# Chunk 0 of a banded-attention and gated-FFN kernel: the second head of each pair is normalized on GpSimd, the first on VectorE

## The chip, the cores and the metric

The kernel runs on one core of one Trainium2 chip. The metric is device time in microseconds (us) of one execution, the median of several runs. The engines are TensorE (PE, with weight loads shown as PEld), VectorE (DVE), ScalarE (ACT), GpSimd (POOL) and SyncE (SP), which issues the loads.

## The reference

Two layers follow each other, all in float32. The first is attention with a narrow band and block summaries: batch 4, 8 heads, 768 positions, head size 64.

```python
k_sum = k.reshape(B, H, nb, block, D).max(axis=3)      # block = 32, nb = 24
v_sum = v.reshape(B, H, nb, block, D).mean(axis=3)
mask_l = np.abs(pos[:, None] - pos[None, :]) < window   # window = 16
scores_l_m = np.where(mask_l, scale * q @ k.T, -1e9)
scores_s = scale * np.einsum('bhsd,bhnd->bhsn', q, k_sum) + np.log(block)
scores_all = np.concatenate([scores_l_m, scores_s], axis=-1)
a = np.exp(scores_all - scores_all.max(-1, keepdims=True))
a = a / (np.sum(a, axis=-1, keepdims=True) + 1e-09)
attn = np.matmul(a, np.concatenate([v, v_sum], axis=2))
```

The second is a feed-forward layer on the eight heads side by side (512 wide, inner width 1024): `h = relu(x @ w_in)`, a convolution of three taps along the positions, a sigmoid gate, and `(h * gate) @ w_out`.

## The kernel before

**Tiling.** The 4 x 768 positions are cut into 8 chunks of 384 (two to a batch element). In a chunk the 8 heads form 4 pairs, so there are 32 pairs, numbered n; pairs 0 to 3 are chunk 0, pairs 4 to 7 chunk 1. A pair goes through `qk` (scores of 64 queries against 96 banded keys and 24 block maxima, in PSUM tiles `pq`), `softmax`, `tr` (each head's scores `a` are transposed on TensorE into the single PSUM tile `pt`, which is copied to SBUF as `aT`) and `av` (product with the values into `xp`, which is split into a high and a low part, `xh` and `xl`).

**Softmax.** For each head and each of three blocks VectorE adds the mask and takes the row maximum (L278), and ScalarE takes the exponential with its row sum (L288). ScalarE then adds 1e-9 to the six sums (L296), VectorE inverts them (L297), and each head's 128 x 360 scores are multiplied by the inverse (L300): the normalization. `n >= NP` sends it to GpSimd from pair 4 on; in chunk 0 VectorE does both heads.

**Feed-forward.** x and both weights are held as a high and a low float32r part, so a product is three matmuls (`f1`, L404; `f2`, L473). `unit` does one of eight slices of the inner width for a chunk: `f1`, then `gate_conv` and `gate_mul`.

**Weights.** They arrive as 64-bit words and are decoded at the start of the kernel: for each of eight blocks of `w_in` (w0 to w7 here) ScalarE scales the high word (L97), VectorE does three integer steps (L100, L101, L104), ScalarE rounds the result to `win_hi` (L127) and GpSimd subtracts it for `win_lo` (L128). The decoded words live in a ring of three buffers `wu`, so L97 of block i waits for L128 of block i-3. In the order listings wu_485, 493, 606, 614, 627, 635, 701 and 709 are w0 to w7.

**Order.** SyncE's loads of chunk 0 follow the list `LOADS`. In chunks 0 and 1 (`ORDERED = 2`) the order of instructions on each engine is set by a scheduler with a cost model of its own, which places all engines' instructions of these chunks; from chunk 2 on TensorE's order is the written one. Within an engine instructions run strictly in order, so an instruction that waits holds all behind it. In chunk 0 matmuls on an idle tile (`warm`, `pw`, L78) fill TensorE's gaps.

Of the kernel before, what the change touches and what calls it, by code (L numbers as in the profile page):

```python
# [25 lines left out]
NP = H // 2  # L26
# [24 lines left out]
def attention_ffn(ctx, tc, qT, kT, vT, v4, w_in, cwT, w_out, mask8, ident_in, out):  # L51
    nc = tc.nc
# [195 lines left out]
    def qk(c, p):  # L248


        st = state[(c, p)]
        n = c * NP + p
        pq = [
            ps.tile([P, 512], F32, tag="s", name=f"pq{n}_{h}", bufs=2) for h in range(2)
        ]
        for blk in range(CB):
            i, half = divmod(blk, 2)
            for h in range(2):
                r = slice(h * QB, (h + 1) * QB)
                last = nc.tensor.matmul(  # L260
                    pq[h][half * QB : (half + 1) * QB, i * NK : (i + 1) * NK],
                    st["q"][r, blk * QB : (blk + 1) * QB],
                    st["kw"][r, blk, :],
                    start=True,
                    stop=True,
                )
        if c == 0:
            warm(f"pq{p}", ins(last))
        softmax(n, c % 2, pq)

    def softmax(n, hf, pq):
        nm = sp.tile([P, 2, 3], F32, tag="nm", name=f"nm{n}", bufs=3)
        sm = sp.tile([P, 2, 3], F32, tag="sm", name=f"sm{n}", bufs=3)
        for h in range(2):
            a = sp.tile([P, 3, NK], F32, tag="a", name=f"a{n}_{h}", bufs=DEPTH + 2)
            state[("a", 2 * n + h)] = a
            for i in range(3):
                nc.vector.tensor_tensor_reduce(  # L278
                    a[:, i, :],
                    pq[h][:, i * NK : (i + 1) * NK],  # L280
                    mask[:, hf, i, :],
                    -0.125,
                    3.0e38,
                    ALU.add,
                    ALU.min,
                    nm[:, h, i : i + 1],
                )
                nc.scalar.activation(  # L288
                    a[:, i, :],
                    a[:, i, :],  # L290
                    AF.Exp,
                    bias=nm[:, h, i : i + 1],
                    scale=-1.0,
                    accum_out=sm[:, h, i : i + 1],
                )
        nc.scalar.activation(sm, sm, AF.Copy, bias=1e-9)  # L296
        nc.vector.reciprocal(sm, sm)  # L297
        for h in range(2):
            a = state[("a", 2 * n + h)]
            (nc.gpsimd if n >= NP else nc.vector).tensor_tensor(  # L300
                a, a, sm[:, h, :].unsqueeze(2).to_broadcast([P, 3, NK]), ALU.mult
            )

# [187 lines left out]
    for item in LOADS.split():  # L491
        what, n = item[0], int(item[1:] or 0)
# [193 lines left out]
```

## Time and profile before

| | us |
|---|---|
| median of 3 runs | 405.03 (401.72 to 405.11) |
| the profiled execution | 405.19 |
| span in its profile | 403.3 |
| TensorE busy | 387.8 (96%) |
| VectorE busy | 262.9 (65%) |
| ScalarE busy | 255.8 (63%) |
| GpSimd busy | 150.3 (37%) |

The span runs from the first to the last instruction; 1.9 us of the execution lie outside it. Busy shares are means over stages with different limits; of TensorE's busy time part is `warm` matmuls, whose results nobody reads.

### The profile page before, as it was taken

What the parts mean: (1) busy time and instruction counts of PE and PEld (TensorE: products, weight loads), DVE (VectorE), ACT (ScalarE), POOL (GpSimd) and SP (SyncE); (2) the same over time, 40 slices, a digit from 0 to 9 for tenths busy, and PEclk for the clock granted to TensorE, in tenths of its full rate; (3) what the DMA queues carried; (4) which work ended last, traced back from release to release, by engine and by line L of the source; (5) the groups of instructions that cost most, each with busy time, mean ns of one, the idle gap of its engine ahead of it and who ended that gap; (6) DMA issues with size and microseconds to landing.
All of it is one profiled execution on the core that took longest, in us unless ns stands there. A gap on an engine that the chain in (4) does not pass through costs nothing.

```text
span 403.3 us, 8835 instructions
## 1 busy us (share of the span) xinstructions
PE 387.8 (96%) x3173; PEld 322.2 (80%) x3173; DVE 262.9 (65%) x777; ACT 255.8 (63%) x806; POOL 150.3 (37%) x179
## 2 busy tenths in 40 slices
PE   8989879999989999999999999999999999999996
PEld 3546558787768888888888888888888888999884
DVE  4889969998976665667765466466565655556200
ACT  3575699998876787766666778666666653343211
POOL 2316565377764234332333333332422242222200
PEclk9999799999899999999999999999999999999999
DMA  8999783666896784546233343334220000000011
GB/s 293 337 367 191 203 212 119 210 199 194 237 205 188 229 261 127 150 148 199 68 101 112 79 114 113 101 98 120 67 63 28 28 2 26 26 28 27 28 52 52
DMA packets 60715, 54.47 MB, mean 135 GB/s; under 512 B 24640, under 2 KB 51328, under 8 KB 60672
## 3 DMA queue, kind: packets, MB, share of 16 engines
q1 hardware_dynamic: 56928, 47.19, 41.2%
q10 hardware_dynamic: 3744, 6.73, 4.5%
q8 instruction: 25, 0.41, 0.5%
q14 instruction: 18, 0.15, 0.1%
HBM read 45.55 MB, written 6.29 MB: 129 GB/s over the span
## 4 chain that ended last, share of the span: by engine, by line
PE 85%; ACT 5%; DVE 3%; DMA 3%; POOL 2%; issue 1%; SPq 0%; DVEq 0%; POOLq 0%
PE f L473 33%; PE f L404 32%; PE pq L260 7%; PE xp L329 5%; PE pt L308 5%; PE pw L78 3%; ACT a L288 2%; DMA va<-v 2%; DMA k_xh<-kT 1%; POOL wout_lo L128 1%; DVE a L300 1%; POOL glo L456 0%; ACT wu_o L97 0%; ACT t L425 0%; PE pv L234 0%
## 5 line engine op out<-in xcount | busy, mean ns | idle before, releaser
L456 POOL TENSOR_TENSOR glo<-t,ghi 128x383 fp32r<-128x383 f32 (+1 forms) x64 | 66.3, 1037 | 138.3 <-ACT ghi L455 125.9
L404 PE MATMUL f<-xh,win_hi 128*128 128x384 f32 (+1 forms) x256 | 92.5, 361 | 0.9 <-ACT win_hi L127 0.9
L434 DVE SCALAR_TENSOR_TENSOR t<-f,cw,t 128x382 f32<-128x382 f32 (+3 forms) x128 | 78.8, 615 | 19.2 <-ACT t L425 16.6
L404 PE MATMUL f<-xl,win_hi 128*128 128x384 f32 (+1 forms) x256 | 87.9, 344 | 0.0
L404 PE MATMUL f<-xh,win_lo 128*128 128x384 f32 (+1 forms) x256 | 87.2, 341 | 0.0
L288 ACT ACTIVATE a<-a,nm 128x120 f32<-128x120 f32 x192 | 73.4, 384 | 12.3 <-DVE nm L278 12.1
L473 PE MATMUL f<-wout_lo,ghi 128*128 128x512 f32 x192 | 75.7, 394 | 1.6 <-POOL wout_lo L128 1.6
L473 PE MATMUL f<-wout_hi,ghi 128*128 128x512 f32 x192 | 76.4, 398 | 0.0
L473 PE MATMUL f<-wout_hi,glo 128*128 128x512 f32 x192 | 75.0, 391 | 0.0
L300 POOL TENSOR_TENSOR a<-a,sm 128x360 f32<-128x360 f32 x56 | 45.7, 837 | 45.6 <-ACT f L422 28.1
L451 ACT ACTIVATE t<-t 128x383 f32<-128x383 f32 (+1 forms) x64 | 33.6, 526 | 40.3 <-DVE t L434 39.6
L452 DVE SCALAR_TENSOR_TENSOR t<-t,f 128x383 f32<-128x383 f32 (+1 forms) x64 | 35.2, 552 | 29.6 <-ACT t L451 29.6
L404 PEld LDWEIGHTS f<-xh,win_hi 128*128 128x128 f32 x256 | 49.3, 192 | 5.1 <-ACT win_hi L127 1.2
L404 PEld LDWEIGHTS f<-xl,win_hi 128*128 128x128 f32 x256 | 49.2, 192 | 1.4 <-issue 0.3
L404 PEld LDWEIGHTS f<-xh,win_lo 128*128 128x128 f32 x256 | 48.9, 191 | 0.2
L278 DVE CUSTOM_DVE_ANT_0 a<-pq,mask 128x120 f32<-128x120 f32 x192 | 42.7, 275 | 1.5 <-PE pq L260 1.3
L473 PEld LDWEIGHTS f<-wout_lo,ghi 128*128 128x128 f32 x192 | 36.1, 188 | 7.9 <-POOL wout_lo L128 2.2
L473 PEld LDWEIGHTS f<-wout_hi,glo 128*128 128x128 f32 x192 | 36.1, 188 | 7.7
L473 PEld LDWEIGHTS f<-wout_hi,ghi 128*128 128x128 f32 x192 | 36.2, 188 | 7.0 <-issue 0.5
L315 ACT COPY aT<-pt 120x384 f32<-120x384 f32 x60 | 28.2, 470 | 20.7 <-PE pt L308 20.7
L422 ACT ACTIVATE f<-f 128x384 f32<-128x384 f32 (+1 forms) x64 | 30.4, 475 | 15.8 <-PE f L404 15.6
L308 PE MATMUL pt<-ident,a 128*120 128x128 f32 x192 | 33.7, 283 | 5.1 <-ACT aT L315 3.1
(59 smaller groups left out, 508.8 us busy)
## 6 DMA issues: line engine op xcount, KB each, us to landing
va<-v SPq DMA_DIRECT2D x32, 288.0 KB, 4.2
kw<-kT SPq DMA_DIRECT2D x28, 288.0 KB, 6.4
q<-qT SPq DMA_DIRECT2D x32, 192.0 KB, 4.5
out_dram<-ob ACTq DMA_DIRECT2D x24, 256.0 KB, 2.0
kT<-kT SPq DMA_DIRECT2D x12, 392.0 KB, 3.9
vt<-vT SPq DMA_DIRECT2D x12, 384.0 KB, 4.3
wo<-w_out SPq DMA_DIRECT2D x8, 512.0 KB, 5.3
raw_a<-w_in SPq DMA_DIRECT2D x6, 512.0 KB, 11.5
```

The costliest lines, as they stand in the source:

```text
L260: last = nc.tensor.matmul(pq[h][half * QB : (half + 1) * QB, i * NK : (i + 1) * NK], st["q"][r, blk * QB : (blk + 1) * QB], st["kw"][r, bl ...
L278: nc.vector.tensor_tensor_reduce(a[:, i, :], pq[h][:, i * NK : (i + 1) * NK], mask[:, hf, i, :], -0.125, 3.0e38, ALU.add, ALU.min, nm[:, h ...
L288: nc.scalar.activation(a[:, i, :], a[:, i, :], AF.Exp, bias=nm[:, h, i : i + 1], scale=-1.0, accum_out=sm[:, h, i : i + 1],)
L300: (nc.gpsimd if n >= NP else nc.vector).tensor_tensor(a, a, sm[:, h, :].unsqueeze(2).to_broadcast([P, 3, NK]), ALU.mult)
L308: last = nc.tensor.transpose(pt[:NK, i * P : (i + 1) * P], a[:, i, :], ident)
L404: last = nc.tensor.matmul(ph[:, :n], w[:, fc, cc, :], x[:, cc, :n], start=(cc == 0 and m == 0), stop=(cc == NCC - 1 and m == 2),)
L422: nc.scalar.activation(h[:, :n], h[:, :n], AF.Relu)
L434: nc.vector.scalar_tensor_tensor(t[:, i0:i1], h[:, hf + k - 1 + i0 : hf + k - 1 + i1], cw[:, fc, k : k + 1], t[:, i0:i1], ALU.mult, ALU.add,)
L451: nc.scalar.activation(t, t, AF.Tanh, scale=0.5)
L452: nc.vector.scalar_tensor_tensor(t, t, 1.0, h[:, hf : hf + ng], ALU.add, ALU.mult)
L456: nc.gpsimd.tensor_tensor(gated["lo"][:, fc, d0 : d0 + ng], t, hi.bitcast(F32), ALU.subtract)
L473: nc.tensor.matmul(po, gx[:, fc, ss], w[:, fc, :], start=(fc == 0 and m == 0), stop=(fc == NFC - 1 and m == 2),)
```

## The change

In `softmax` the test that picks the engine of the normalization gets `or h`: in chunk 0, too, GpSimd now multiplies the scores of the second head (h = 1) of each pair. That is four instructions. Nothing else is edited.

```diff
         for h in range(2):
             a = state[("a", 2 * n + h)]
-            (nc.gpsimd if n >= NP else nc.vector).tensor_tensor(
+            (nc.gpsimd if n >= NP or h else nc.vector).tensor_tensor(
                 a, a, sm[:, h, :].unsqueeze(2).to_broadcast([P, 3, NK]), ALU.mult
             )
```

The scheduler reacts to it with another order of both ordered chunks on every engine. Three places matter below.

ScalarE, between the second and the fourth pair of chunk 0, before (a_0_364 and a_1_371 are the two heads of pair 3, wu_i_485 and wu_i_493 are w0 and w1):

```order
L315 COPY aT_307<-pt_301 120x384
L296 ACTIVATE sm_275<-sm_275 128x6
L236 ACTIVATE vm_2_298<-pv_2_296 24x128
L349 CAST xh_325<-xp_309 128x384
L97 ACTIVATE cw<-cw_words 128x24
L97 ACTIVATE wu_i_485<-raw_a 128x512
L97 ACTIVATE wu_i_493<-raw_a 128x512
L288 ACTIVATE a_0_364,sm_363<-a_0_364,nm_362 128x120 x3
L288 ACTIVATE a_1_371,sm_363<-a_1_371,nm_362 128x120 x3
```

The same place on ScalarE now:

```order
L296 ACTIVATE sm_275<-sm_275 128x6
L315 COPY aT_307<-pt_301 120x384
L97 ACTIVATE wu_i_493<-raw_a 128x512
L349 CAST xh_325<-xp_309 128x384
L97 ACTIVATE wu_i_606<-raw_a 128x512
L127 CAST win_hi<-wu_i_493 128x512
L97 ACTIVATE wu_i_614<-raw_a 128x512
L236 ACTIVATE vm_3_386<-pv_3_384 24x128
L288 ACTIVATE a_0_364,sm_363<-a_0_364,nm_362 128x120 x3
L288 ACTIVATE a_1_371,sm_363<-a_1_371,nm_362 128x120 x3
```

The exponentials of pair 3 stood behind the first step of w0 and w1; now they stand behind that of w1, w2 and w3 and behind the finished w1.

VectorE, ahead of the first masked maximum of pair 4 (a_0_540), before:

```order
L344 CAST xl_748<-xl_326 128x4x2
L101 SCALAR_TENSOR_TENSOR wu_i_614<-wu_i_614,wl_i_615 128x512
L104 SCALAR_TENSOR_TENSOR wu_i_614<-raw_a,wu_i_614 128x512
L100 TENSOR_SCALAR wl_i_628<-raw_a 128x512
L101 SCALAR_TENSOR_TENSOR wu_i_627<-wu_i_627,wl_i_628 128x512
L104 SCALAR_TENSOR_TENSOR wu_i_627<-raw_a,wu_i_627 128x512
L100 TENSOR_SCALAR wl_i_636<-raw_a 128x512
L278 ISA a_0_540,nm_538<-pq_0_524,mask 128x120
```

VectorE at the same place now (xp_462 is the attention output of pair 3):

```order
L104 SCALAR_TENSOR_TENSOR wu_i_635<-raw_a,wu_i_635 128x512
L100 TENSOR_SCALAR wl_i_702<-raw_b 128x512
L101 SCALAR_TENSOR_TENSOR wu_i_701<-wu_i_701,wl_i_702 128x512
L350 TENSOR_TENSOR xl_326<-xp_462,xh_325 128x384
L104 SCALAR_TENSOR_TENSOR wu_i_701<-raw_b,wu_i_701 128x512
L100 TENSOR_SCALAR wl_i_710<-raw_b 128x512
L344 CAST xh_747<-xh_325 128x4x2
L344 CAST xl_748<-xl_326 128x4x2
L101 SCALAR_TENSOR_TENSOR wu_i_709<-wu_i_709,wl_i_710 128x512
L278 ISA a_0_540,nm_538<-pq_0_524,mask 128x120
```

Before, w0 to w4 and the first step of w5 were decoded when pair 4's softmax began; now w0 to w6 and two steps of w7 are.

GpSimd in the first half of chunk 0, before and now in one piece of the difference (va are the values' block means, kw_107 the keys of pair 3, the ISA row loads a function library):

```order
 L217 COPY kw_100<-ks_243 128x6x24
 L238 COPY va_104<-vm_0_175 24x768
+L300 ISA
+L300 TENSOR_TENSOR a_1_160<-a_1_160,sm_152 128x360
+L300 TENSOR_TENSOR a_1_217<-a_1_217,sm_209 128x360
+L238 COPY va_111<-vm_1_232 24x768
+L238 COPY va_116<-vm_2_298 24x768
 L213 COPY kw_107<-k_xl 128x6x96
-L238 COPY va_111<-vm_1_232 24x768
 L217 COPY kw_107<-ks_331 128x6x24
```

The two normalizations and two copies of block means now stand ahead of pair 3's keys; the library load, which stood ahead of the first L128, now stands ahead of the first L300.

## Rows read from the trace of the kernel before

**Rows 1.** The page: its head, part 1 (busy us, share, instructions), and the granted clock of part 2 in 40 slices.

```profile
span 403.3 us, 8835 instructions
PE 387.8 (96%) x3173; PEld 322.2 (80%) x3173; DVE 262.9 (65%) x777; ACT 255.8 (63%) x806; POOL 150.3 (37%) x179
...
PEclk9999799999899999999999999999999999999999
```

**Rows 2.** Busy time of each engine in stretches of 10 us, then the granted clock (1.00 is 2.4 GHz), the DMA share and GB/s.

```profile
40.00:50.00 10.00, 8.05 (x61) 5.53 (x51) 9.21 (x33) 6.12 (x29) 5.78 (x5) 0.74 0.70 197
50.00:60.00 10.00, 7.06 (x96) 5.44 (x95) 6.77 (x28) 9.11 (x30) 5.69 (x7) 0.92 0.85 222
60.00:70.00 10.00, 10.00 (x95) 8.09 (x94) 9.26 (x29) 9.35 (x32) 5.93 (x8) 1.00 0.38 119
...
100.00:110.00 10.00, 9.45 (x56) 7.43 (x57) 10.00 (x24) 8.60 (x27) 7.47 (x7) 0.83 0.84 220
```

**Rows 3.** TensorE in order of time: start, duration, operation, count, and in brackets the idle time ahead and what ended it.

```profile
43.54 0.83 PE L260 MATMUL pq<-kw,q 64*64 64x120 f32 x12 [1.95 <-issue]
...
59.74 0.52 PE L308 MATMUL pt<-ident,a 128*120 128x128 f32 x3 [2.79 <-ACT aT L315]
...
60.80 0.44 PE L404 MATMUL f<-xh,win_hi 128*128 128x384 f32 x1
...
101.75 0.50 PE L473 MATMUL f<-wout_lo,ghi 128*128 128x512 f32 x1 [0.54 <-POOL wout_lo L128]
...
111.95 0.50 PE L473 MATMUL f<-wout_lo,ghi 128*128 128x512 f32 x1 [1.03 <-POOL wout_lo L128]
```

**Rows 4.** The normalization by line: engine, count, ns shortest/median/longest, first and last start.

```profile
L300 POOL TENSOR_TENSOR a<-a,sm x56: 777/790/1333, 46.8 to 325.5; 128x360 f32<-128x360 f32 x56
L300 DVE TENSOR_TENSOR a<-a,sm x8: 521/604/1153, 12.6 to 28.8; 128x360 f32<-128x360 f32 x8
```

**Rows 5.** VectorE in order of time: the four pairs of normalizations of chunk 0, and the first masked maximum of pair 3.

```profile
12.63 1.64 DVE L300 TENSOR_TENSOR a<-a,sm 128x360 f32<-128x360 f32 x2
...
17.26 1.12 DVE L300 TENSOR_TENSOR a<-a,sm 128x360 f32<-128x360 f32 x2
...
21.72 1.60 DVE L300 TENSOR_TENSOR a<-a,sm 128x360 f32<-128x360 f32 x2
...
24.18 0.27 DVE L278 CUSTOM_DVE_ANT_0 a<-pq,mask 128x120 f32<-128x120 f32 x1
...
28.35 0.97 DVE L300 TENSOR_TENSOR a<-a,sm 128x360 f32<-128x360 f32 x2
```

**Rows 6.** VectorE in order of time: the three steps of one undisturbed block of weights, the instructions that took longer than their like, the split of pair 3's attention output (L350), and the first masked maximum of pair 4.

```profile
30.30 0.42 DVE L100 TENSOR_SCALAR wl_i<-raw_a 128x512 uint32<-128x512 uint32 x1
30.76 0.69 DVE L101 SCALAR_TENSOR_TENSOR wu_i<-wu_i,wl_i 128x512 uint32<-128x512 uint32 x1
31.48 0.69 DVE L104 SCALAR_TENSOR_TENSOR wu_i<-raw_a,wu_i 128x512 uint32<-128x512 uint32 x1
...
33.70 1.65 DVE L101 SCALAR_TENSOR_TENSOR wu_i<-wu_i,wl_i 128x512 uint32<-128x512 uint32 x1
...
35.99 0.55 DVE L350 TENSOR_TENSOR xl<-xp,xh 128x384 fp32r<-128x384 f32 x1
...
36.79 0.16 DVE L344 CAST xh<-xh 128x8 fp32r<-128x8 f32 x1
36.87 1.28 DVE L344 CAST xl<-xl 128x8 fp32r<-128x8 f32 x1
...
40.63 1.65 DVE L104 SCALAR_TENSOR_TENSOR wu_i<-raw_a,wu_i 128x512 uint32<-128x512 uint32 x1
...
42.65 0.27 DVE L278 CUSTOM_DVE_ANT_0 a<-pq,mask 128x120 f32<-128x120 f32 x1
```

**Rows 7.** GpSimd in order of time over the same stretch.

```profile
31.57 3.24 POOL L128 TENSOR_TENSOR win_lo<-wu_i,win_hi 128x512 fp32r<-128x512 f32 x2 [3.11 <-ACT win_hi L127]
...
36.80 1.31 POOL L128 TENSOR_TENSOR win_lo<-wu_i,win_hi 128x512 fp32r<-128x512 f32 x1 [1.29 <-ACT win_hi L127]
...
40.19 1.54 POOL L128 TENSOR_TENSOR win_lo<-wu_i,win_hi 128x512 fp32r<-128x512 f32 x1 [1.29 <-DMA va<-v]
```

**Rows 8.** ScalarE in order of time: the copy of pair 3's first transposed head, then from the first exponential of pair 4 to the copy that frees `pt` at 59.6 us.

```profile
30.42 0.48 ACT L315 COPY aT<-pt 120x384 f32<-120x384 f32 x1 [2.00 <-PE pt L308]
...
42.96 0.40 ACT L288 ACTIVATE a<-a,nm 128x120 f32<-128x120 f32 x1
...
49.92 0.48 ACT L315 COPY aT<-pt 120x384 f32<-120x384 f32 x1 [2.23 <-PE pt L308]
...
50.41 0.61 ACT L127 CAST win_hi<-wu_i 128x512 fp32r<-128x512 f32 x1
50.91 0.48 ACT L422 ACTIVATE f<-f 128x384 f32<-128x384 f32 x1
52.28 0.48 ACT L315 COPY aT<-pt 120x384 f32<-120x384 f32 x1 [0.89 <-PE pt L308]
...
53.13 0.62 ACT L127 CAST win_hi<-wu_i 128x512 fp32r<-128x512 f32 x1
53.64 0.70 ACT L97 ACTIVATE wu_i<-raw_b 128x512 f32<-128x512 f32 x1
...
59.11 0.49 ACT L315 COPY aT<-pt 120x384 f32<-120x384 f32 x1
```

## The prediction

> **What bounds the kernel now.** I read the page's head first: TensorE is busy for 387.8 of 403.3 us, and its granted clock is below 0.9 in two of the 40 slices only [rows 1]. So a saving must take idle time, `warm` matmuls or slow-clock time from TensorE; work taken off another engine counts only through these. The table of 10 us stretches tells where that is possible [rows 2]. From 60 us on TensorE is full (10.00 of 10); between 40 and 60 it has 8.05 and 7.06, and the granted clock, 0.74 and 0.92, says that part of that time ran at the 1.2 GHz level. The four moved instructions lie before this point, so the question is when TensorE gets past it. I take the matmul group on `pt` at 59.74 as the checkpoint: behind it stands the first wide feed-forward matmul, at 60.80, and after that TensorE is fed nearly without a gap [rows 3]. A shift of the checkpoint is a shift of the end, unless something later gives it back.
>
> What sets the checkpoint? The matmul at 59.74 waits for ScalarE's copy of 59.11, the last of a chain on ScalarE that begins with pair 4's first exponential at 42.96 [rows 8]. That one needs pair 4's first masked maximum, which VectorE runs at 42.65 as the next item of a full queue (9.21 of 10 us busy between 40 and 50) [rows 2, 6]. So: VectorE's queue up to 42.65, then ScalarE's chain, then the checkpoint.
>
> **The change part by part.**
>
> *Relief.* The four pairs of normalizations cost VectorE 1.64 + 1.12 + 1.60 + 0.97 = 5.33 us [rows 5]. Half goes: -2.7 us.
>
> *Order.* The listing of VectorE now has more decoding ahead of pair 4's maximum: two steps of w5 (0.69 + 0.69 less overlap, 1.3), all three of w6 (1.8) and two of w7 (1.2), by the three durations of an undisturbed block [rows 6]: +4.3 us.
>
> *Interference.* Three instructions took far longer than their like while GpSimd was at an L128: 1.65 for 0.69 (33.70), 1.28 for 0.16 (36.87), 1.65 for 0.69 (40.63), together 3.0 us [rows 6]; GpSimd worked 3.24 + 1.31 + 1.54 = 6.1 us there [rows 7]. VectorE lost half of GpSimd's time. In the new order six L128 at about 1.3 us (7.8) and four normalizations at 0.79 (3.2) [rows 4, 7] come before pair 4's maximum, 11.0 us, half of which is 5.5: +2.5 over before. The bounds are no loss beyond today's (0) and the loss of all 11.0 us (+8). I take the half, because it is what this stage shows.
>
> VectorE's own sum: 42.65 - 2.7 + 4.3 + 2.5 = 46.75, between 44.25 and 52.25.
>
> *A second path to the same place.* The split of pair 3's output (L350) now stands ahead of pair 4's maximum, so VectorE also waits for pair 3. Pair 3's maximum was at 24.18 [rows 5]. Ahead of it now are w0, w1 and two steps of w2 (3.6 + 1.2 = 4.8); three pairs' relief is -2.2, and interference from one L128 and three normalizations (1.3 + 3 x 0.79, halved) is +1.8: 28.6. From there to pair 3's normalization I keep roughly the distance of before (28.35 - 24.18 = 4.2), with 1.2 for the larger ScalarE queue, in which the exponentials stand behind the first step of w1 to w3: 34.0. From normalization to L350's end took 36.5 - 28.35 = 8.2 us [rows 5, 6], which gives 42.2. But the copy of the first transposed head, 2.1 us behind the normalization before (30.42) [rows 8], now stands on ScalarE behind the first step of w6, which waits in the ring for GpSimd's L128 of w3. That is 34.0 + 0.5 + 0.8 + 0.3 for GpSimd to reach it, two L128 at 1.3 and 0.7 for the step itself (L97 took 0.70 [rows 8]): 38.9, and 39.4 with the copy, 3.3 later than its old distance. So L350 ends at 45.5. Behind it stand the last of w6, two steps of w7 and the casts, 2.0 us, and half an L128, 0.65: **pair 4's maximum at 48.1**. The later of the two paths counts, 5.5 us behind 42.65.
>
> *What ScalarE gives back.* From pair 4's first exponential to the copy's end it took 59.60 - 42.96 = 16.64 us. Of that, 2.23 + 0.89 were waits for TensorE [rows 8], which a later start absorbs. Two L127 (0.61, 0.62), the L422 and an L97 (0.70) stood in between; they were done earlier or come later in the new order, about 2.1 us net of overlap. That leaves 11.4. The checkpoint is then 48.1 + 0.3 + 11.4 + 0.14 = 59.9, against 59.74: +0.2. Pair 4's score tiles and `pt` are shared by alternating pairs, and such hand-overs have left gaps of 1.95 and 2.79 us on TensorE [rows 3]; I allow a part, 0.8. **Front: +1.0 us.**
>
> *Middle.* In chunk 1 the new order puts the first `f2` matmuls behind unit 3, whose 12 `f1` matmuls take some 2.1 us. The waits for `wout_lo` of 0.54 and 1.03 [rows 3] are then mostly covered: -0.8. At best the slow clock there goes too (9.45 us busy at 0.83 [rows 2], so 1.7 us) and it is -3.3; if the moved unit waits itself, +1.
>
> *Costs taken at nothing.* The library load moves from before the first L128 to before the first L300. Its time shows in no row; it lies between 0 and the 3.11 us that GpSimd waited there anyway [rows 7]. Now the first head's transposition, behind a matmul on block means that comes later, covers it; without that cover up to 3 us of pair 0 are lost, ahead of VectorE's queue and so mostly absorbed there. The second head's 0.79 us on GpSimd runs beside VectorE's half, and a pair took 0.97 to 1.64 on VectorE alone [rows 4, 5]: no later. SyncE's loads keep their list.
>
> **Sum.** 405.19 (the profiled execution, 0.16 above the median, 1.9 of it outside the span) + 1.0 - 0.8 = **405.4 us**.
>
> *Where a page speaks against it.* A normalization took 777 to 1333 ns on GpSimd and 521 to 1153 on VectorE, by the medians 790 to 604, a ratio of 1.3 [rows 4]. The Trainium skill, "GPSIMD Engine Reference", section 4.1 (Engine selection), puts elementwise work with two inputs at about twice VectorE's time. By that the four would take some 1.2 us more on GpSimd than I count, and half of that, 0.6 us, would return to VectorE (an estimate from that page); the measured 790 ns decides here.
>
> **The rivals.**
>
> *A. Slower: GpSimd's instructions hold VectorE for their whole length.* The place is VectorE's queue up to pair 4's maximum; the price is the upper bound above, 52.25, then 0.3 + 11.4 + 0.14: checkpoint 64.1, +4.4, so 409.6 without the middle's gain. It decides once VectorE loses over 9 of the 11 us. For it: each of the three long instructions is an elementwise one that ran beside an L128. Against it: other instructions ran at their usual length in GpSimd's 6.1 us, and only half was lost [rows 6, 7]. By the Trainium skill, "SBUF — State Buffer", section "SBUF: two separate sides", the two engines share a port pair under an exclusive lock, held for a whole instruction, with the loser blocked. The three long rows agree with that; the ordinary ones between them show that not every VectorE instruction asks for it. Chance 0.15.
>
> *B. Faster: the relief gets through.* Were the interference no more than before and pair 3 in time, pair 4's maximum comes at 44.25 and the checkpoint at 44.25 + 0.3 + 11.4 + 0.14 = 56.1, -3.6 us; with the middle 400.8, at best 398.3. For it: 2.7 us really leave a queue that is full. Against: the decoding moved ahead of it is larger, and the ring's wait behind pair 3 is new. Chance 0.13.
>
> *C. Slower by the clock.* Between 40 and 50 us, with idle stretches such as the 1.95 at 43.54, TensorE was granted 0.74 [rows 2, 3]. If the later pair 4 moves such a stretch into 50 to 60, where 7.06 us ran at 0.92, the work there takes about 3 us longer with no gap to absorb it: 405.4 + 3 = 408.4. Chance 0.10.
>
> That the change does not do what it says is out: the listings show the four instructions on GpSimd.
>
> **How the numbers follow.** My forecast has 0.62, A 0.15, B 0.13, C 0.10. One per cent, 4 us, is about what a measurement of this kernel can tell from no change. Faster than 401.0: most of B and a little of the forecast with the middle's best end, 0.14. Slower than 409.1: most of A, part of C and the forecast's tail if the interference is nearer its upper bound, 0.24. Within: 0.62. The range runs from 401.0, just above B, to 409.4, just below A, and leaves out about 2 in 10.
>
> **What would show it.** On VectorE four L300 instead of eight before 50 us, pair 4's first maximum near 48 (44 is B, 52 is A), and more L101, L104 or casts of over 1.2 us. On ScalarE an L97 waiting for GpSimd's L128 just before pair 3's `aT`. On TensorE the `pt` group that waits for `aT` near 60, the clock of 50 to 60 near 0.92 (C: 0.7), and smaller waits for `wout_lo` after 100. I would be wrong if the block of w_in decoding takes much longer through the ring than its parts (each step waits for another engine), if pair 3's weights for ScalarE arrive late and hold its exponentials, or if the new order of chunk 1 opens gaps on TensorE after 60 us, which the rows of before cannot show.

## The result and the profile after

The changed kernel takes 406.39 us (median of 20 runs, 405.68 to 407.16), the kernel before 404.94 in the same comparison (20 runs, 401.41 to 406.59). The ratio is 1.0057, with a 95% interval of 1.0035 to 1.0079: slower by half a per cent, inside the 1% that the forecast (405.4) called no change, and inside its range. In every comparison, executions more than 1.5% above the fastest of the same kernel count as slow and are left out of the ratio. The profiled execution took 405.68 us, so the profiles stand 0.5 us apart and the medians 1.45.

The page of the changed kernel, its head, part 1 and the granted clock of part 2:

```profile
span 403.8 us, 8837 instructions
PE 384.4 (95%) x3163; PEld 319.4 (79%) x3173; DVE 262.6 (65%) x773; ACT 256.5 (64%) x806; POOL 152.9 (38%) x183
...
PEclk9999999999999999999999999999999999999999
```

Against [rows 1], four instructions have gone from DVE (777 to 773) to POOL (179 to 183), and TensorE is busy 3.4 us less in a span 0.5 us longer. The ten matmuls fewer are records that this trace lacks, all of `warm` (75 against 85, with 3173 weight loads in both), so part of the 3.4 us is theirs. What differs where, the 10 us stretches tell (PE, PEld, DVE, ACT, POOL busy, then granted clock, DMA share, GB/s):

```profile
10.00:20.00 10.00, 6.57 (x50) 3.50 (x51) 7.92 (x31) 5.98 (x28) 5.25 (x8) 0.93 1.07 340
20.00:30.00 10.00, 9.45 (x102) 5.76 (x101) 9.86 (x32) 6.46 (x22) 5.30 (x6) 0.90 1.05 373
30.00:40.00 10.00, 7.17 (x53) 4.26 (x52) 9.62 (x15) 6.38 (x17) 6.63 (x7) 1.00 0.94 195
40.00:50.00 10.00, 8.89 (x104) 6.20 (x105) 9.37 (x38) 7.14 (x28) 5.46 (x6) 1.00 0.51 137
50.00:60.00 10.00, 9.59 (x102) 7.63 (x103) 6.30 (x27) 9.51 (x35) 5.80 (x8) 1.00 1.11 260
...
100.00:110.00 10.00, 7.63 (x57) 5.22 (x57) 10.00 (x22) 8.93 (x27) 7.57 (x7) 1.00 0.78 242
```

Between 40 and 60 TensorE is busier and at full clock, where before it had 8.05 at 0.74 and 7.06 at 0.92 [rows 2]. It pays at other places, 10 to 20 and 30 to 40, of which the kernel before had

```profile
10.00:20.00 10.00, 10.00 (x104) 5.81 (x104) 8.79 (x35) 5.38 (x28) 3.11 (x6) 1.00 1.07 337
...
30.00:40.00 10.00, 9.14 (x97) 6.67 (x100) 9.68 (x17) 5.53 (x10) 6.04 (x5) 1.00 0.98 200
```

and 100 to 110 (9.45 at 0.83 before [rows 2]). TensorE of the changed kernel in order of time shows the first and the last of them, and the checkpoint between them:

```profile
18.26 0.28 PE L234 MATMUL pv<-ident,vs 128*24 128x128 f32 x1 [3.12 <-DVE vs L228]
...
57.62 0.52 PE L308 MATMUL pt<-ident,a 128*120 128x128 f32 x3 [0.26 <-ACT aT L315]
...
99.75 0.50 PE L473 MATMUL f<-wout_hi,ghi 128*128 128x512 f32 x1 [1.15 <-ACT wout_hi L127]
...
101.10 0.50 PE L473 MATMUL f<-wout_lo,ghi 128*128 128x512 f32 x1 [0.30 <-POOL wout_lo L128]
...
108.69 0.50 PE L473 MATMUL f<-wout_lo,ghi 128*128 128x512 f32 x1 [1.95 <-POOL wout_lo L128]
...
116.38 0.50 PE L473 MATMUL f<-wout_lo,ghi 128*128 128x512 f32 x1 [0.51 <-POOL wout_lo L128]
...
120.91 0.50 PE L473 MATMUL f<-wout_lo,ghi 128*128 128x512 f32 x1 [0.36 <-POOL wout_lo L128]
```

The checkpoint, 59.74 before [rows 3], is at 57.62, 2.1 us earlier. The end is 0.5 us later, so 2.6 us went behind it: the waits for `wout_hi` and `wout_lo` are 4.3 us here (3.15 in a second profile of this kernel, `after_again`), against 0.54 and 1.03 for `wout_lo` [rows 3]. And at 18.26 stands a wait that the kernel before does not have, 3.12 us for pair 2's block mean; behind it the granted clock is 0.67 in 18 to 20 and 0.50 in 20 to 22 us, where the kernel before was granted 1.00.

VectorE in order of time, the instructions named in the steps and those that took longer than their like:

```profile
17.25 0.95 DVE L228 TENSOR_REDUCE vs<-raw_b 128x24 f32<-128x768 f32 x1 [1.47 <-DMA raw_b<-vT]
...
19.17 1.19 DVE L101 SCALAR_TENSOR_TENSOR wu_i<-wu_i,wl_i 128x512 uint32<-128x512 uint32 x1
...
23.37 1.26 DVE L300 TENSOR_TENSOR a<-a,sm 128x360 f32<-128x360 f32 x1
...
24.55 1.27 DVE L101 SCALAR_TENSOR_TENSOR wu_i<-wu_i,wl_i 128x512 uint32<-128x512 uint32 x1
...
28.40 0.28 DVE L278 CUSTOM_DVE_ANT_0 a<-pq,mask 128x120 f32<-128x120 f32 x1
...
30.22 1.05 DVE L100 TENSOR_SCALAR wl_i<-raw_a 128x512 uint32<-128x512 uint32 x1
...
33.25 1.00 DVE L300 TENSOR_TENSOR a<-a,sm 128x360 f32<-128x360 f32 x1
...
34.63 1.29 DVE L100 TENSOR_SCALAR wl_i<-raw_a 128x512 uint32<-128x512 uint32 x1
...
36.03 1.58 DVE L101 SCALAR_TENSOR_TENSOR wu_i<-wu_i,wl_i 128x512 uint32<-128x512 uint32 x1
...
42.28 0.56 DVE L350 TENSOR_TENSOR xl<-xp,xh 128x384 fp32r<-128x384 f32 x1
...
42.76 1.22 DVE L104 SCALAR_TENSOR_TENSOR wu_i<-raw_b,wu_i 128x512 uint32<-128x512 uint32 x1
...
45.14 0.28 DVE L278 CUSTOM_DVE_ANT_0 a<-pq,mask 128x120 f32<-128x120 f32 x1
```

The block mean at 17.25 waits 1.47 us for its load, and TensorE waits for the block mean. Pair 4's first maximum stands at 45.14. ScalarE in order of time, the places of [rows 8] and the ring:

```profile
35.68 0.71 ACT L97 ACTIVATE wu_i<-raw_a 128x512 f32<-128x512 f32 x1 [1.66 <-POOL win_lo L128]
...
37.09 0.67 ACT L97 ACTIVATE wu_i<-raw_b 128x512 f32<-128x512 f32 x1 [0.70 <-DMA va<-vm]
...
37.68 0.46 ACT L315 COPY aT<-pt 120x384 f32<-120x384 f32 x1
...
45.46 0.40 ACT L288 ACTIVATE a<-a,nm 128x120 f32<-128x120 f32 x1 [0.45 <-DVE nm L278]
...
57.01 0.47 ACT L315 COPY aT<-pt 120x384 f32<-120x384 f32 x1
```

### The profile page after: what moved, and what is told of

Its sections match the earlier page's. It is cut to its first block, busy times and chain, and to the rows that moved or that the text cites. A ratio compares the mean times of both kernels' runs of the same rounds, so it can differ in the third digit from the quotient of the medians.

```text
span 403.8 us, 8837 instructions
## 1 busy us (share of the span) xinstructions
PE 384.4 (95%) x3163; PEld 319.4 (79%) x3173; DVE 262.6 (65%) x773; ACT 256.5 (64%) x806; POOL 152.9 (38%) x183
## 4 chain that ended last, share of the span: by engine, by line
PE 72%; DVE 12%; ACT 6%; DMA 5%; POOL 3%; issue 1%; SPq 1%; DVEq 0%; POOLq 0%
PE f L473 32%; PE f L404 27%; PE xp L329 5%; PE pt L308 4%; PE pq L260 4%; ACT a L288 3%; DMA raw_b<-vT 2%; DVE wu_i L101 2%; DMA k_xl<-kT 2%; DMA q<-qT 1%; DVE wu_i L104 1%; DVE t L434 1%; POOL wout_lo L128 1%; DVE wl_i L100 1%; DVE wu_o L101 1%; POOL glo L456 1%
## 5 line engine op out<-in xcount | busy, mean ns | idle before, releaser
L404 PE MATMUL f<-xh,win_hi 128*128 128x384 f32 (+1 forms) x256 | 90.9, 356 | 0.2 <-ACT xh L349 0.2
L300 POOL TENSOR_TENSOR a<-a,sm 128x360 f32<-128x360 f32 x60 | 48.1, 821 | 43.8 <-ACT f L422 28.0
L404 PEld LDWEIGHTS f<-xh,win_hi 128*128 128x128 f32 x256 | 48.2, 189 | 4.8 <-issue 1.1
L404 PEld LDWEIGHTS f<-xl,win_hi 128*128 128x128 f32 x256 | 48.3, 189 | 1.4
L404 PEld LDWEIGHTS f<-xh,win_lo 128*128 128x128 f32 x256 | 48.1, 188 | 0.6 <-issue 0.3
L315 ACT COPY aT<-pt 120x384 f32<-120x384 f32 x60 | 28.1, 468 | 17.2 <-PE pt L308 17.2
L455 ACT CAST ghi<-t 128x383 fp32r<-128x383 f32 (+1 forms) x64 | 32.6, 509 | 8.6 <-DVE t L452 8.3
```

What stands on the lines that cost most here:

```text
L300: (nc.gpsimd if n >= NP or h else nc.vector).tensor_tensor(a, a, sm[:, h, :].unsqueeze(2).to_broadcast([P, 3, NK]), ALU.mult)
L315: nc.scalar.copy(aT[:NK, :], pt[:NK, : 3 * P])
L404: last = nc.tensor.matmul(ph[:, :n], w[:, fc, cc, :], x[:, cc, :n], start=(cc == 0 and m == 0), stop=(cc == NCC - 1 and m == 2),)
L455: nc.scalar.copy(hi, t)
```

## The experiments

The diff changes the engine of four instructions and, through the scheduler, the order of everything in chunks 0 and 1. To set the two apart, most kernels below carry a function that chains each engine's instructions in a listed order after tracing, by order alone and with no wait:

```diff
     with tile.TileContext(nc) as tc:
         attention_ffn(tc, *args, o)
+        replay(nc, tc)
```

"Old order" is the list of the kernel before, "new order" that of the changed one. Theories: **Interference** (a term of the prediction's front: what VectorE is relieved of, contention with GpSimd takes back), **Order** (the new order costs time whatever the engine), and two narrower ones that came up on the way, **Load** (the new order queues ready work behind a block mean whose load has not landed) and **Clock** (the kernel before has a stretch at the low clock, which the change trades for waits).

### Order and engine apart

`before_again` is the kernel before with no edit (an empty diff), as the measure of the spread.

> The kernel before once more, unchanged, to see what its single executions do: the 20 so far spread from 401.4 to 406.6 us, while those of the changed kernel lie between 405.7 and 407.2. Theory Clock: the spread is the TensorE clock; executions near 401.5 us show a mean granted clock of about 0.995, those near 405 to 406 show 0.985 to 0.988, as the profiled one did (0.987). Theory Waits: the spread comes from engines and transfers, the clock is the same in all of them.

It took 403.85 us (401.78 to 406.39, 12 runs), ratio 0.9989 (0.9955 to 1.0022). With 12 runs an interval of this kernel is about 0.33% to either side. Its executions bear out the clock's part of the spread: three at 0.996 took 401.78 to 402.25 us, seven at 0.986 and 0.987 took 403.6 to 406.4, though one at 1.000 took 402.79.

`old_order_split` makes the change and keeps the old order:

```diff
-            (nc.gpsimd if n >= NP else nc.vector).tensor_tensor(
+            (nc.gpsimd if n >= NP or h else nc.vector).tensor_tensor(
...
+        replay(nc, tc)
```

> The order of before is kept on every engine; only the four normalizations of the second heads go to GpSimd, at the places in its order that they had in time. Theory Order (the scheduler's new order, not the four instructions, made the result): VectorE is relieved by 2.7 us and loses about 0.5 to GpSimd, pair 4's first masked maximum comes near 40.5 us instead of 42.65, and the time is 402 to 404 us if TensorE can use it. Theory Split (the four instructions on GpSimd cost what they save): pair 4's maximum stays at 42.5 or later, and the time is 405 to 407 us.

It took 405.15 us (402.97 to 408.52), ratio 1.0023 (0.9988 to 1.0058): no gain is seen in the old order, as its Split theory had said. Its VectorE in order of time:

```profile
13.26 0.95 DVE L228 TENSOR_REDUCE vs<-raw_b 128x24 f32<-128x768 f32 x1 [0.68 <-DMA raw_b<-vT]
...
15.13 0.95 DVE L210 TENSOR_REDUCE ks<-k_xl 128x24 f32<-128x768 f32 x1 [0.93 <-DMA k_xl<-kT]
...
20.56 0.95 DVE L228 TENSOR_REDUCE vs<-raw_b 128x24 f32<-128x768 f32 x1 [2.25 <-DMA raw_b<-vT]
...
44.48 0.27 DVE L278 CUSTOM_DVE_ANT_0 a<-pq,mask 128x120 f32<-128x120 f32 x1
```

Relieved of four instructions, VectorE arrives early at three block summaries and waits 3.86 us for their loads. Pair 4's maximum is no earlier than 42.65 [rows 6] but later. That need not be the split's doing: pair 2's values came late in this execution, TensorE, too, waits 1.43 us for their block mean, at 21.57, is granted 0.83 in 20 to 30 us (1.00 before), and VectorE then waits 1.19 us for pair 3's scores. `before_short_out` (below), the same front with all eight on VectorE, shows the same where the values came late: a wait of 1.74 us at 22.02, 0.83 in 20 to 30, and the maximum at 44.30. In this execution loads paced the front of chunk 0 as much as VectorE did, which the prediction did not count.

`new_order_dve` is the counterpart: the new order, with all eight on VectorE.

```diff
-            (nc.gpsimd if n >= NP or h else nc.vector).tensor_tensor(
+            (nc.gpsimd if n >= NP else nc.vector).tensor_tensor(
...
+        replay(nc, tc)
```

> The order of the changed kernel on every engine, but all eight normalizations on VectorE, the second head's right behind the first's. Theory Order: VectorE gets 2.7 us back and loses 0.5 us less to GpSimd, pair 4's first masked maximum comes near 47.3 us instead of 45.1, and the time is 1 to 2 us above the changed kernel, 407 to 408.5 us. Theory Split: the time is that of the changed kernel or lower, 404.5 to 406.4 us.

It took 408.56 us (407.73 to 410.81), ratio 1.0097 (1.0065 to 1.013). So the order alone costs 1%, 4 us. Pair 4's maximum in its profile, at 46.11, stands 1.0 us behind that of the changed kernel, but not behind those of the other profiles with the new front and the split (45.90, 46.15 and 47.23), so it does not show where the 2 us between the two kernels arise.

In the new order the four instructions do win on GpSimd: 1.0097 against 1.0057 (and 1.0037 in a second comparison, below) is 1.6 to 2.4 us, and no execution of the one kernel reaches into those of the other. In the old order no gain is seen. The change is the sum of that order's cost of 4 us and of a gain of 2 that is seen only in it. The two prices hold for this way round: with the split first, it costs 0.9 us (not clear of noise) and the order then 0.6 to 1.4.

### In which chunk the order costs

`new_then_old` (split) and `old_then_new` (no split) change the list at about 74 us, where both orders have run the same instructions on every engine. The edits are those of `old_order_split` and of `new_order_dve`'s last line, with the two lists joined.

> The changed kernel with its own order up to 74 us (all of chunk 0's attention) and the order of before from there on, on every engine; both orders have run the same instructions by then. In the changed kernel TensorE stood 1.3 us ahead there and ended 0.5 us behind in the profiled executions. Theory Order: the lead is kept, and the time is 1.5 to 2.5 us under the changed kernel, 403.9 to 404.9 us. Rival Given back: the weights of the second layer hold TensorE in either order, the lead turns into longer waits for them, and the time is 405.7 to 406.7 us.

407.05 us (404.79 to 408.32), ratio 1.0058 (1.0032 to 1.0085): as slow as the whole change, although the old order follows. Order had expected 403.9 to 404.9, and missed; its rival's 405.7 to 406.7 came nearer. Its TensorE waits for `wout_lo` as before, not as after:

```profile
103.08 0.50 PE L473 MATMUL f<-wout_lo,ghi 128*128 128x512 f32 x1 [0.54 <-POOL wout_lo L128]
...
113.15 0.80 PE L473 MATMUL f<-wout_lo,ghi 128*128 128x512 f32 x1 [2.43 <-POOL wout_lo L128]
```

> The kernel before (all normalizations on VectorE) in its own order up to 74 us, and in the changed kernel's order from there on. If the new order of chunk 1 is what costs, the time is 1 to 2.5 us above before, 405.5 to 407 us. If what is behind 74 us is equally good in both orders, and the loss lies ahead of it, the time is that of before within 0.7 us, 404 to 405.5 us.

404.55 us (403.0 to 408.09), ratio 1.0015 (0.9979 to 1.0051). It has the waits of the new order for `wout_hi` and `wout_lo` (1.12, 0.31, 0.77, 0.50 and 0.36 us) and yet measures like the kernel before. Together the two point to chunk 0's order for the cost, though their intervals overlap. The comparison of two profiles above had said the contrary (checkpoint 2.1 us early, 2.6 us lost behind it).

That the checkpoint of one execution says little about an order shows in this kernel's own TensorE row:

```profile
57.09 0.51 PE L308 MATMUL pt<-ident,a 128*120 128x128 f32 x3 [2.02 <-ACT aT L315]
```

It runs the same front as the kernel before, with 57.09 for 59.74. Over the profiles at hand the old front without the split gave 57.09, 59.71, 59.74 and 61.36, the new one with it 57.62, 58.39, 58.64 and 59.71. So the new front costs time at the end without a later checkpoint; where TensorE loses it is not shown.

### The waits for w_out

If the waits around 100 to 120 us are the cost, a shorter decoding of `w_out` must take it away. Both kernels got it: the first two VectorE steps of each `w_out` block cover 8 of 512 columns, so the output is not the reference's.

```diff
-        nc.vector.tensor_scalar(low, lo_word, 29, None, ALU.logical_shift_right)
+        m = 8 if name[0] == "o" else n
+        nc.vector.tensor_scalar(
+            low[:, :m], lo_word[:, :m], 29, None, ALU.logical_shift_right
+        )
         nc.vector.scalar_tensor_tensor(
-            out, out, 3, low, ALU.logical_shift_left, ALU.bitwise_or
+            out[:, :m], out[:, :m], 3, low[:, :m], ALU.logical_shift_left, ALU.bitwise_or
         )
```

> The kernel before in its own order; for the eight blocks of w_out, VectorE's first two decoding steps run over 8 of 512 columns, so these weights are not fully decoded, and VectorE has about 1 us less to do per block. Theory Given back (in either order TensorE's waits for the low part of w_out between 98 and 121 us absorb what the front gains or loses): the waits of 0.54 and 1.03 to 2.4 us there go, and the time is 1 to 2 us under before, 402.5 to 403.5 us. Rival: the waits stay, since ScalarE and GpSimd set them, 404 to 405 us.

403.16 us (401.52 to 406.32), ratio 0.9967 (0.9935 to 0.9999). Theory Given back forecast the time, but not the row it was to come from: in the profile, of the longest of the 12 executions, the waits stand as before.

```profile
104.60 0.50 PE L476 MATMUL f<-wout_lo,ghi 128*128 128x512 f32 x1 [0.49 <-POOL wout_lo L131]
...
113.09 0.50 PE L476 MATMUL f<-wout_lo,ghi 128*128 128x512 f32 x1 [1.11 <-POOL wout_lo L131]
```

> The changed kernel in its own order, with the same shortened decoding of w_out as before_short_out. Theory Given back: its waits of 1.15, 0.30, 1.95, 0.50 and 0.36 us go, its lead in the front (1.3 us at 74 us) shows, and it is level with or up to 1.5 us faster than before_short_out: 401 to 403 us. Rival (the new order loses elsewhere, or the loads eat its lead): it stays 1 to 3 us slower than before_short_out, 404 to 406 us.

404.39 us (403.08 to 406.23), ratio 0.9987 (0.9958 to 1.0016), in the range of its rival, 404 to 406. Its waits for `w_out` shrank to 0.31, 0.89 and 0.50 us, but the early one stayed, as its TensorE shows (lines are shifted by 3 in both shortened kernels):

```profile
19.26 0.28 PE L237 MATMUL pv<-ident,vs 128*24 128x128 f32 x1 [3.90 <-DVE vs L231]
...
106.85 0.50 PE L476 MATMUL f<-wout_lo,ghi 128*128 128x512 f32 x1 [0.89 <-POOL wout_lo L131]
```

The kernel before gains 1.3 us by its ratio (0 to 2.6), the changed one some 1.9 against its two medians, and 1.2 us still lie between their medians, with intervals that overlap. So the decoding of `w_out` is in the path of both. That the waits for it are what it costs is not shown: the shorter steps also relieve VectorE, which before was busy for all of 100 to 110 [rows 2], and in the kernel before the rows of the waits did not shrink. Nor is it shown that they make the change's cost.

### The early load wait

`after_again` is the changed kernel with no edit, run beside the next one.

> The changed kernel once more, unchanged, beside the next two. Loads that land later than in its first profile (pair 2's values at 17.2 us there, 18.2 to 20.5 in other runs) should show here as a longer wait of TensorE ahead of pair 2's block means (3.12 us there) and a later first masked maximum of pair 4 (45.1 us there). Time 405.7 to 407.5 us.

406.24 us (405.68 to 407.12), ratio 1.0037 (1.0017 to 1.0057). Its TensorE has the early wait in two parts:

```profile
18.32 0.28 PE L234 MATMUL pv<-ident,vs 128*24 128x128 f32 x1 [1.87 <-DVE vs L228]
...
21.66 0.54 PE L308 MATMUL pt<-ident,a 128*120 128x128 f32 x3 [1.64 <-DVE aT L313]
```

`new_softmax_first` keeps the new order but lets pair 2's softmax and the transpositions go ahead of its block mean, the decoding of `cw` and the start of that of w0, on all engines but SyncE. On VectorE the list moves so (vs_2_294 is the block mean of pair 2, a_1_283 pair 2's second head):

```diff
 L278 ISA nm_274 128x1
-L228 TENSOR_REDUCE vs_2_294<-raw_b 128x24
-L100 TENSOR_SCALAR wl_cw<-cw_words 128x24
...
 L313 COPY aT_253<-pt_247 120x384
 L278 ISA a_1_283,nm_274<-pq_1_258,mask 128x120
...
 L278 ISA nm_274 128x1
+L228 TENSOR_REDUCE vs_2_294<-raw_b 128x24
+L100 TENSOR_SCALAR wl_cw<-cw_words 128x24
```

> The changed kernel with one place of its order mended: the block means of pair 2 and the first weights' decoding, which wait for loads at about 16 to 18 us, go behind the softmax of pair 2 and behind the transpositions of pairs 0 and 1 on every engine (there the order of before put them). Theory Loads (the new order puts work that waits for loads ahead of work that is ready): TensorE's wait of 3.1 to 3.9 us for the block means of pair 2 falls under 1.5 us, pair 4's first masked maximum comes 1.5 to 2.5 us earlier than in after_again, and the time is 1 to 2.5 us lower, 404 to 405.4 us. Theory Given back: the front is earlier, the end is not, within 0.7 us of after_again.

404.67 us (404.45 to 405.93), ratio 1.0005 (0.9979 to 1.003). Of its 12 runs only two (405.75 and 405.93) reach above the lowest of `after_again`'s (405.68): this placement is worth 1.6 us. Its TensorE:

```profile
19.15 0.27 PE L234 MATMUL pv<-ident,vs 128*24 128x128 f32 x1
...
24.38 0.28 PE L234 MATMUL pv<-ident,vs 128*24 128x128 f32 x1 [2.42 <-DVE vs L228]
...
26.41 0.89 PE L308 MATMUL pt<-ident,a 128*120 128x128 f32 x3 [1.75 <-DVE aT L313]
```

Pair 2's block mean is not waited for any more (19.15); the same pattern one pair later now is (24.38). Pair 4's maximum moved from 45.90 in `after_again` to 44.74, 1.2 us where Load had forecast 1.5 to 2.5. The waits of TensorE shown for the two kernels add up to 3.5 us in `after_again` and 4.2 here, so TensorE does not wait less there; that the gain comes from ready work being done earlier is a reading that no run tests by itself.

`new_mended` does the same for pair 3: its softmax, too, goes ahead of the decoding. On ScalarE, for one:

```diff
+L288 ACTIVATE a_0_364,sm_363<-a_0_364,nm_362 128x120 x3
+L288 ACTIVATE a_1_371,sm_363<-a_1_371,nm_362 128x120 x3
 L127 CAST win_hi<-wu_i_485 128x512
 L97 ACTIVATE wu_i_493<-raw_a 128x512
...
-L288 ACTIVATE a_0_364,sm_363<-a_0_364,nm_362 128x120 x3
-L288 ACTIVATE a_1_371,sm_363<-a_1_371,nm_362 128x120 x3
```

> As new_softmax_first, with the same mending carried on through chunk 0: the softmax of pair 3 goes ahead of what waits for the loads of pair 3's values and of the third and fourth block of w_in, ScalarE's copy of pair 3's first transposed head ahead of the sixth block's first step (which waits in the ring for GpSimd), and pair 4's masked maxima ahead of the last block's decoding. new_softmax_first still had TensorE waiting 2.42 us for pair 3's block means and 1.75 us behind it. Theory Loads: these waits go too, pair 4's first masked maximum comes near 42.5 us (44.7 there), and the time is 1 to 2 us under new_softmax_first, 402.7 to 403.7 us, under both kernels. Theory Given back: the front is earlier and the waits for the low part of w_out between 98 and 121 us grow by as much, 404 to 405 us.

408.69 us (407.88 to 410.5), ratio 1.0116 (1.0068 to 1.0164): a miss, 4 us above `new_softmax_first`. Its ScalarE shows one fault, a cast that waits with the next block's first step queued behind it:

```profile
36.91 0.62 ACT L127 CAST win_hi<-wu_i 128x512 fp32r<-128x512 f32 x1 [2.85 <-DVE wu_i L104]
37.44 0.67 ACT L97 ACTIVATE wu_i<-raw_a 128x512 f32<-128x512 f32 x1
```

VectorE then waits 0.92 us for that step, and pair 4's maximum comes 2.3 us later than in `new_softmax_first`:

```profile
38.14 1.29 DVE L101 SCALAR_TENSOR_TENSOR wu_i<-wu_i,wl_i 128x512 uint32<-128x512 uint32 x1 [0.92 <-ACT wu_i L97]
...
47.01 0.28 DVE L278 CUSTOM_DVE_ANT_0 a<-pq,mask 128x120 f32<-128x120 f32 x1 [0.91 <-PE pq L260]
```

Written by hand, the second move put a ring hand-over in the wrong order. Its granted clock is also low, 0.72 in 30 to 40 and 0.83 in 40 to 50 us, and 0.979 to 0.986 over its six executions; how the 4 us divide was not taken apart. It says nothing against Load at pair 3, which stays open.

`old_split_v2_first` attacks the load itself: `old_order_split` with pair 2's values requested ahead of w0.

```diff
 L193 DMA va_111<-v 96x6x128
+L179 DMA raw_b<-vT 128x768
 L110 DMA raw_a<-w_in 128x1024
-L179 DMA raw_b<-vT 128x768
```

> As old_order_split (order of before, second heads on GpSimd), with one load moved: the values of pair 2 go ahead of the first block of w_in. In old_order_split VectorE waited 2.25 us for them at 20.56 us, so that all it had been relieved of was gone at 21.7 us. Theory Loads (up to 22 us the loads, not VectorE, set the pace, and relief becomes waiting): the wait falls under 1 us, pair 4's first masked maximum comes before 43.3 us (44.48 there), and the time is 1 to 2 us under old_order_split, 403 to 404.2 us. Theory Split: nothing is won, 404.8 to 406 us.

405.66 us (402.35 to 408.57), ratio 1.0023 (0.9987 to 1.0059). Its Loads theory missed (403 to 404.2, pair 4's maximum before 43.3), and Split's 404.8 to 406 holds. VectorE's wait for pair 2's values fell from 2.25 to 0.34 us and pair 4's maximum came at 43.70, 0.8 earlier than in `old_order_split`, but still behind the 42.65 of the kernel before; 1.54 us of waiting for pair 3's values, at 25.46, are new. So one earlier load does not set free what VectorE is spared, and why the old order shows no gain stays open.

### The clock of the kernel before

`old_gap_warm` keeps the kernel before and puts eight more `warm` matmuls into the gap ahead of 43.54 [rows 3].

```diff
-WARM = {"start": 10, "pq0": 5, "pq1": 12, "pq2": 3, "pq3": 3, "tr": 2, "av": 3, "unit": 3}
+WARM = {"start": 18, "pq0": 5, "pq1": 12, "pq2": 3, "pq3": 3, "tr": 2, "av": 3, "unit": 3}
...
+        replay(nc, tc)
```

> The kernel before in its own order, with eight more idle-tile (warm) matmuls on TensorE in the gap of 1.95 us ahead of 43.54 (the first scores of pair 5); the matmul that follows cannot start earlier either way. Theory Clock (the spread of the kernel before is the slow clock that follows TensorE's gaps, the largest piece of it the 6.8 us at the 1.2 GHz level from 44.7 us on): that stretch stays at full clock, the mean granted clock is 0.992 or more in nearly all executions, and the median is 401.8 to 403 us against about 404.6 for before. Rival: the slow stretch only comes later, behind one of the gaps after 100 us, and the time is 404 to 405 us.

404.16 us (401.81 to 406.38), ratio 0.9986 (0.9954 to 1.0018). Its stretches, with columns as above:

```profile
40.00:50.00 10.00, 8.40 (x79) 5.50 (x77) 9.81 (x35) 9.15 (x35) 6.66 (x7) 1.00 0.92 233
50.00:60.00 10.00, 7.58 (x84) 6.17 (x85) 9.25 (x37) 9.80 (x38) 6.12 (x7) 0.83 0.73 190
```

40 to 50, at 0.74 before, now runs at the full clock, and pair 4's maximum is at 41.21; but the next stretch drops to 0.83, and 100 to 110 is at 0.83 too. The mean clock was 0.990 or more in all 12 executions, about as forecast. The time was not: 404.16 lies above Clock's 401.8 to 403 and in its rival's 404 to 405, where the slow stretch only comes later. A gain of up to 0.5% is left open by the interval.

## Why the prediction was right, and where its steps were not

The number held: 405.4 forecast, 406.39 measured, a difference of 1.0 us. But the sum (+1.0 in front, -0.8 in the middle) came near for partly wrong reasons. In the profiles the front is -2.1 (59.74 to 57.62) and all behind it +2.6: both terms had the wrong sign and nearly cancelled, as the forecast's terms did with the signs the other way. That much is luck. Of the prediction's own signs the four L300 and the L97 that waits for GpSimd came; the checkpoint near 60, the clock near 0.92 in 50 to 60, the smaller waits for `wout_lo` and more than the three L101, L104 or casts of over 1.2 us did not.

- **The place.** Chunk 0's front decides: the two joined orders point to it for the cost, and not to chunk 1. A front that costs time is right by these runs, but not by the way that was forecast: the checkpoint was to come at 59.9, or 60.7 with the allowance, and no profile of the new front with the split has it later than 59.71. That a shift of the checkpoint is a shift of the end did not hold: more was given back behind it than it had gained.
- **Relief: -2.7, measured -2.0.** The four normalizations left on VectorE took 0.53 + 0.53 + 1.26 + 1.00 = 3.32 us of the 5.33. The step halved a time that itself held stretched instructions.
- **Interference: +2.5, measured +1.0. This term was mis-sized.** Beside the normalizations, whose stretch is in the relief, six stretched rows stand above (1.19 at 19.17 to 1.22 at 42.76). Each less its undisturbed duration (0.42 for L100, 0.69 for L101 and L104 [rows 6]), they lost 4.0 us; before, the three long ones lost 3.0. With the stretch of the normalizations it is 5.2 against 4.5. GpSimd's L128 and L300 ahead of the maximum came to 12.6 us instead of the 11.0 counted (the four L300 took 1.03, 1.14, 1.08 and 0.79), twice the 6.1 of before, and the loss grew by a sixth, with the normalizations counted on both sides, or by a third without: half of GpSimd's time, which fitted three rows, is not the law. The sum also left out GpSimd's copies: the rows at 19.17 and 30.22 are stretched beside copies (L238 at 18.91 and 29.69, L213 at 19.88), not beside an L128 or L300. Rival A needed more than 9 of 11 us and is out. The Trainium skill, "SBUF — State Buffer", section "SBUF: two separate sides", has an exclusive lock by which one of the two engines is blocked for a whole instruction, and which only certain VectorE instructions ask for. The rows agree in kind: while an L128 ran from 28.08 to 29.62, the masked maxima, which read PSUM, kept their 0.28 us.
- **VectorE's sum and the second path.** 46.75 and 48.1 were forecast for pair 4's maximum; it was 45.14 and 45.90 in the two profiles of the changed kernel. Along the second path, pair 3's maximum came at 28.40 (28.6 forecast), its normalization at 33.25 (34.0), the ring's wait for GpSimd ahead of its `aT` copy is there (1.66 at 35.68 for w5's first step, and w6's, at 37.09, begins as the L128 that GpSimd started at 34.37 end), and the copy at 37.68 (38.9). Its last piece, L350's end at 42.84, was forecast at 45.5: behind the copy 6.1 us were counted and 4.7 were needed. Of the 1.4 us, 0.5 is a slip in the sum, which takes the new copy's end against the old copy's start.
- **ScalarE's chain: 11.4, measured 57.48 - 45.46 = 12.0.** Right, within 0.6; the allowance of 0.8 for hand-overs covers them.
- **Middle: -0.8, and this step had the wrong sign in the profile.** The first `f2` did move, but the waits for `w_out` grew to 4.3 us. They end when the decoding of `w_out` ends, so an earlier TensorE only waits longer: that is how I read the loss of the checkpoint's 2.1 us behind it, from this one pair of profiles; it was not tested by itself. That the decoding of `w_out` is worth time is shown by the two shortened kernels; that the new order of chunk 1 costs little or nothing, by `old_then_new` (at most 0.5% by its interval).
- **What was missing.** No step looked at the loads of chunk 0. The new order puts pair 2's block mean, whose load had not landed, ahead of ready work; TensorE waited 3.12 us at 18.26, and the granted clock was 0.50 in 20 to 22. Undoing that placement won 1.6 us, which is about all of the difference to the kernel before in that comparison. And beside the sum, the 1.2 us that the prediction estimates for slower normalizations are 1.7 by its own numbers, twice 604 ns against 790; nothing rests on them.
- **Rivals B and C.** B (faster) did not happen: even without the new order the split shows no gain (`old_order_split`). C's low clock between 50 and 60 is not there: 1.00.

Open remain two things. Of the 1% that the new order costs without the split, 1.6 us are traced to one placement, if it is worth as much without the split as with it; the rest, how the front's cost reaches the end, and why the split wins 2 us in that order, were not taken apart, since `new_mended` failed for a reason of its own. And no version beat both kernels: the best of the changed ones, `new_softmax_first`, equals the kernel before.

## What to carry to other kernels

Where a scheduler sets the order, an edit is two changes, the instructions and the new order; replaying either order with either edit (four kernels) prices them separately, and here they were +4 and -2 us, taken in this sequence. Before counting what a relieved engine wins, look at what it waits for when it arrives early: in the profile of the split in the old order VectorE waited 3.86 us for three loads. And a milestone in one profile is not a property of an order: the same front gave checkpoints from 57.1 to 61.4 us.

## What the runs showed of the hardware

**A load's landing varies more than the effect under study.** Pair 2's values, with the same place in SyncE's list, became usable between 17.2 us and 21.0 us in the ten profiles in which VectorE waited for them. SyncE had asked for them at 9.15 to 9.98 us, the latest landing belonging to the latest request: the difference grew on the way from 0.8 to 3.8 us.

**The spread of the kernel before follows its granted clock.** In the comparison with `after_again` its 29 runs fall apart by the mean clock of the execution: five at 0.996 took 401.5 to 401.84 us, one at 0.991 took 402.6, and 23 at 0.985 to 0.987 took 403.6 to 406.5. The changed kernel's runs took 405.7 to 407.1 at any clock from 0.987 to 0.996. At an equal 0.996 the two kernels are thus over 4 us apart there, not 1.5. In the two other comparisons with many runs of before the order is looser: its executions at 0.996 took 401.6 to 402.6 and 402.0 to 403.8. My reading, which no run tests, is that most executions of the kernel before have a stretch at 1.2 GHz that the changed one does not pay for in the same way, and that what such a stretch costs depends on where it falls. In the profile of before the later of its two was at 100 to 110 (0.83 [rows 2], in 104 to 106 the 0.50 that is 1.2 GHz) with a wait for `wout_lo` of 1.03 after it [rows 3]. In `before_again` it came a stretch later:

```profile
100.00:110.00 10.00, 8.81 (x60) 6.61 (x60) 10.00 (x24) 8.84 (x28) 7.87 (x7) 1.00 0.80 229
110.00:120.00 10.00, 8.21 (x66) 6.44 (x66) 6.92 (x20) 6.03 (x20) 5.89 (x6) 0.83 0.90 199
```

and there TensorE's wait stood ahead of it:

```profile
111.79 0.50 PE L473 MATMUL f<-wout_lo,ghi 128*128 128x512 f32 x1 [2.44 <-POOL wout_lo L128]
```

Here 0.50 was granted in 114 to 116. That span was 404.4 us against 403.3. In the one profile the low clock fell ahead of the wait, and the wait was 1.4 us shorter; in the other it fell behind, and the end came 1.1 us later. This is read from two profiles and was not tested by itself; why an execution of the kernel before at 0.996 takes 401.5 us was not seen, since none of them was profiled.
